# A retention and token-mixing kernel: 64-row PE tiles for two chunks at a time, in an explicit order of steps

## The chip, the cores and the metric

The kernel runs on one core of a Trainium2 chip. The metric is device time in microseconds (us) of one launch. A profile of one execution gives the span, engine times and waits. The timed figure of the profiled execution lies 1.7 to 1.8 us above its span, so spans are compared with spans and times with times.

Runs of one kernel differ by some per cent. The slower ones often show a lower clock granted to TensorE (PE), as with the changed kernel's 119.21 us at 0.927 of full clock against 114.94 us at 0.940, but not always: a fast run of e13, 115.26 us, had 0.888. Where the text says half clock, PE was granted half of its full clock for a while (0.50 from 30 to 35 us in the trace of the changed kernel). A run more than 1.5% above the fastest of the same kernel is labelled slow.

## The reference, cut to what matters

```python
# q, k, v: (B=4, H=8, S=768, D=64) float32
gamma = 1.0 - 2.0 ** (-5.0 - np.arange(H))
for t in range(S):                                   # retention with decay
    state = gamma * state + outer(k[:, :, t], v[:, :, t])
    y[:, :, t] = (1 / sqrt(D)) * q[:, :, t] @ state
x  = y as (B, S, H * D)                              # 512 columns
wq, wk = x @ w_q, x @ w_k                            # 64 columns each
W_tok  = (1 / sqrt(64)) * einsum('bsd,btd->bst', wq, wk)
mixed  = einsum('bst,btd->bsd', W_tok, x)
return maximum(mixed, 0) @ w_out                     # (4, 768, 512)
```

Both kernels take the recurrence in chunks of 128 tokens. q is multiplied by gamma^t and k by gamma^-t; then each chunk is masked scores times v, plus q times the state of all earlier chunks. `mixed` is computed as wq (wk^T x), so z = wk^T x (64 x 512) comes first, once per batch, and no S x S matrix is formed.

## The kernel before

24 chunks, one after another, placed by a scheduler. One 256 KB load for each of q, k and v in a chunk, in rows of one head and one token:

```python
nc.sync.dma_start(
    out=q_st,                                        # [128 tokens, H, D] float32
    in_=q[b, :, c * C : (c + 1) * C, :].rearrange("h t d -> t h d"),
)
# ... k and v alike ...
nc.gpsimd.tensor_tensor(out=qs, in0=st["q_st"],
    in1=fq[:, c, :].to_broadcast([128, H, D]), op=ALU.mult)
# ... ks alike, on GpSimd ...
nc.scalar.activation(out=vs, in_=st["v_st"], func=ACT.Copy, scale=float(attn_scale))
```

Transposes (8 for a chunk), scores in two 64-row tiles, mask, state and output:

```python
for parity in range(2):
    ps = psum_pool.tile([128, 4, C], FP32, name="at_ps", tag="ps")
    for j in range(4):
        h = 2 * j + parity
        nc.tensor.matmul(out=ps[:, j, :], lhsT=kT(qkt, h), rhs=qT(qkt, h), ...)
# ... at_sb = at_ps * cmask on DVE, twice 128 x 512 ...
for hp in range(HP):                                 # both heads of a pair in one 128 x 128 product
    nc.tensor.matmul(out=state_ps[:, hp, :, :], lhsT=ks[:, 2*hp : 2*hp+2, :],
                     rhs=vs[:, 2*hp : 2*hp+2, :], ...)
nc.scalar.copy(out=u_tile[0:64, :, 0, :], in_=state_ps[0:64, :, 0, :])       # keep the two
nc.scalar.copy(out=u_tile[64:128, :, 1, :], in_=state_ps[64:128, :, 1, :])   # diagonal blocks
# ... y_ps: 4 matmuls qkt x u_tile, 8 matmuls at_sb x vs ...
```

The mixing stage of a batch (wq and wk products, z, mx, projection with w_out) is placed beside the attention of the next batch. All tiles in PSUM come from one pool of eight buffers.

## Time and profile before

| | before |
|---|---|
| time, median of 3 runs | 132.82 us (132.27 to 135.31) |
| span | 132.4 us |
| PE busy, matmuls | 97.8 us, 1128 |
| DVE, ACT, POOL busy | 78.6, 58.3, 50.9 us |
| packets of DMA | 79,933 |

Busy time of PE counts the modelled lengths of matmuls that overlap; it is not the time PE needs. For that one goes from start to start in the timeline, as the prediction does. Two lines that the prediction does not show matter later. The first is from the list of DMA queues (packets, MB, share of 16 engines), the second from the groups of instructions (line, engine, operation, tiles, count, then busy us and mean ns, then idle time before them):

```profile
q8 instruction: 9, 0.15, 0.4%
...
L221 DVE TENSOR_TENSOR at_sb<-at_ps,cmask 128x512 bf16<-128x512 f32 x48 | 31.0, 684 | 25.0 <-PE at_ps L211 25.0
```

Queue q8 is labelled "instruction": nine packets of 16 KB, 0.15 MB in all, while PE runs 2256 instructions.

### The profile page before, as it was taken

To read this page: it belongs to the slowest core of one execution; us is meant where nothing else is said; L and a number is where in the kernel's file an instruction comes from. 1 tells how busy PE (TensorE), PEld (TensorE's weight loads), DVE (VectorE), ACT (ScalarE), POOL (GpSimd) and SP (SyncE) were. 2 spreads that over 40 slices of the span, in tenths; PEclk is the share of its full clock that TensorE was granted. 3 is DMA by queue.
4 is the path that set the end of the run, shared out by engine and by line. 5 is a ranking of instruction groups with operands and counts; after the bars stand their busy time and mean duration, and the time that the engine had idled before them with its cause. 6 is when DMAs were issued, how large, how long until landed. Compare 5 with 4: busy or idle time off the path is not lost.

```text
span 132.4 us, 2906 instructions
## 1 busy us (share of the span) xinstructions
PE 97.8 (74%) x1128; PEld 64.1 (48%) x1128; DVE 78.6 (59%) x141; ACT 58.3 (44%) x127; POOL 50.9 (38%) x65
## 2 busy tenths in 40 slices
PE   0003679765699899981799899861999999977970
PEld 0002558544478466560476556541675556653320
DVE  4061654975767599393457797590637797551830
ACT  3002454653556645382315757362325657413430
POOL 4009755467627654240765550425754200000000
PEclk9999999999999999999779999998569999999999
DMA  3899999999979998959999839959998006600074
GB/s 83 289 272 247 240 245 228 225 246 246 270 168 229 240 226 261 237 168 272 254 244 251 196 83 303 251 172 268 260 223 197 0 4 235 241 0 0 5 296 179
DMA packets 79933, 26.66 MB, mean 201 GB/s; under 512 B 76336, under 2 KB 76336, under 8 KB 79920
## 3 DMA queue, kind: packets, MB, share of 16 engines
q1 hardware_dynamic: 79920, 26.48, 79.6%
q8 instruction: 9, 0.15, 0.4%
q14 instruction: 4, 0.03, 0.1%
HBM read 20.19 MB, written 6.29 MB: 200 GB/s over the span
## 4 chain that ended last, share of the span: by engine, by line
PE 52%; SPq 16%; DMA 13%; ACT 4%; DVE 4%; POOL 4%; issue 3%; POOLq 0%; ACTq 0%; DVEq 0%
PE o_ps L379 13%; DMA q_st<-in_q_dram 12%; SPq L142 6%; PE wqt_ps L308 6%; PE z_ps L342 5%; PE mx_ps L358 4%; PE at_ps L211 4%; SPq L134 4%; PE tr_ps L181 3%; PE xt_ps L285 3%; PE y_ps L269 3%; SPq L138 3%; POOL qs L156 3%; PE wk_ps L322 3%; PE y_ps L261 3%
## 5 line engine op out<-in xcount | busy, mean ns | idle before, releaser
L221 DVE TENSOR_TENSOR at_sb<-at_ps,cmask 128x512 bf16<-128x512 f32 x48 | 31.0, 684 | 25.0 <-PE at_ps L211 25.0
L156 POOL TENSOR_TENSOR qs<-q_st,fq 128x512 bf16<-128x512 f32 x24 | 25.0, 1042 | 48.2 <-DMA q_st<-in_q_dram 33.3
L276 ACT CAST x_nat<-y_ps 128x512 bf16<-128x512 f32 x24 | 14.0, 585 | 29.5 <-PE y_ps L269 29.4
L162 POOL TENSOR_TENSOR ks<-k_st,fk 128x512 bf16<-128x512 f32 x24 | 25.0, 1042 | 3.6 <-DMA k_st<-in_k_dram 2.5
L181 PE MATMUL tr_ps<-identity,qs 128*128 128x128 bf16 x96 | 10.5, 239 | 20.4 <-POOL qs L156 20.3
L379 PE MATMUL o_ps<-wout_sb,relu_mx 128*128 128x512 bf16 x96 | 22.4, 379 | 0.0
L199 DVE COPY qkt<-tr_ps 128x1024 bf16<-128x1024 bf16 x24 | 16.4, 681 | 4.3 <-PE tr_ps L190 4.3
L181 PEld LDWEIGHTS <-qs 128*128 128x128 bf16 x96 | 6.9, 106 | 23.7 <-POOL qs L156 21.6
L168 ACT ACTIVATE vs<-v_st 128x512 bf16<-128x512 f32 x24 | 15.2, 632 | 0.3 <-DMA v_st<-in_v_dram 0.3
L367 DVE TENSOR_SCALAR relu_mx<-mx_ps 128x512 bf16<-128x512 f32 x16 | 9.9, 683 | 8.0 <-PE mx_ps L358 8.0
L379 PEld LDWEIGHTS <-relu_mx 128*128 128x128 bf16 x96 | 8.9, 98 | 9.8 <-DVE relu_mx L367 1.1
L238 PE MATMUL state_ps<-vs,ks 128*128 128x128 bf16 x80 | 8.6, 232 | 4.8 <-ACT vs L168 2.8
L190 PE MATMUL tr_ps<-identity,ks 128*128 128x128 bf16 x96 | 10.7, 242 | 1.1 <-POOL ks L162 1.1
L269 PE MATMUL y_ps<-vs,at_sb 128*128 128x64 bf16 x192 | 11.1, 201 | 0.0
L247 ACT CAST u_tile<-state_ps 64x256 bf16<-64x256 f32 x20 | 7.3, 365 | 8.3 <-PE state_ps L238 8.3
L211 PE MATMUL at_ps<-qkt 64*128 64x128 bf16 x192 | 10.6, 233 | 0.4 <-DVE qkt L199 0.4
L285 PE MATMUL xt_ps<-identity,x_nat 128*128 128x128 bf16 x96 | 10.0, 228 | 1.2 <-ACT x_nat L276 1.1
L388 DVE COPY o_st<-o_ps 128x512 f32<-128x512 f32 x12 | 8.2, 686 | 3.8 <-PE o_ps L379 2.1
L390 ACT COPY o_st<-o_ps 128x512 f32<-128x512 f32 x12 | 7.0, 584 | 7.3 <-PE o_ps L379 5.7
L308 PE MATMUL wqt_ps<-x_t,wq_sb 128*64 128x256 bf16 x48 | 9.2, 342 | 0.3 <-DVE x_t L296 0.3
L238 PEld LDWEIGHTS <-ks 128*128 128x128 bf16 x80 | 5.9, 105 | 7.1 <-issue 7.0
L261 PE MATMUL y_ps<-u_tile,qkt 128*128 128x128 bf16 x80 | 9.3, 226 | 0.0
(37 smaller groups left out, 101.1 us busy)
## 6 DMA issues: line engine op xcount, KB each, us to landing
q_st<-in_q_dram SPq DMA_DIRECT2D x24, 256.0 KB, 4.3
k_st<-in_k_dram SPq DMA_DIRECT2D x24, 256.0 KB, 4.2
v_st<-in_v_dram SPq DMA_DIRECT2D x24, 256.0 KB, 4.3
out_dram<-o_st SPq DMA_DIRECT2D x24, 256.0 KB, 2.3
wout_stage<-in_moe_w_out_dram SPq DMA_DIRECT2D x1, 1024.0 KB, 5.9
wq_stage<-in_moe_w_q_dram SPq DMA_DIRECT2D x1, 128.0 KB, 2.2
wk_stage<-in_moe_w_k_dram SPq DMA_DIRECT2D x1, 128.0 KB, 2.4
```

Source lines behind the costliest of these rows:

```text
L156: nc.gpsimd.tensor_tensor(out=qs, in0=st["q_st"], in1=fq[:, c, :].to_broadcast([128, H, D]), op=ALU.mult,)
L162: nc.gpsimd.tensor_tensor(out=ks, in0=st["k_st"], in1=fk[:, c, :].to_broadcast([128, H, D]), op=ALU.mult,)
L168: nc.scalar.activation(out=vs, in_=st["v_st"], func=ACT.Copy, scale=float(attn_scale))
L181: nc.tensor.matmul(out=tr_ps[:, hp, :], lhsT=qs[:, 2 * hp : 2 * hp + 2, :], rhs=identity, is_transpose=True, start=True, stop=True,)
L199: nc.vector.tensor_copy(out=qkt, in_=tr_ps)
L211: nc.tensor.matmul(out=ps[:, j, :], lhsT=kT(qkt, h), rhs=qT(qkt, h), start=(j == 0), stop=(j == 3),)
L221: nc.vector.tensor_tensor(out=at_sb_par[:, parity, :, :], in0=at_ps[parity], in1=cmask.to_broadcast([128, 4, C]), op=ALU.mult,)
L238: nc.tensor.matmul(out=state_ps[:, hp, :, :], lhsT=ks[:, 2 * hp : 2 * hp + 2, :], rhs=vs[:, 2 * hp : 2 * hp + 2, :], start=(c == 0 and hp ...
L269: nc.tensor.matmul(out=y_ps[:, h, :], lhsT=at_sb[:, h, :], rhs=vs[:, h, :], start=(c == 0 and h == 0), stop=(h == H - 1),)
L276: nc.scalar.copy(out=x_nats[b][:, c, :], in_=y_ps)
L308: nc.tensor.matmul(out=wqt_ps, lhsT=wq_sb[:, dmc, :], rhs=x_t[:, dmc, blk * 2 * C : (blk + 1) * 2 * C], start=(dmc == 0), stop=(dmc == NDM ...
L379: nc.tensor.matmul(out=o_ps, lhsT=relu_mx[:, dmc, tc_i * C : (tc_i + 1) * C], rhs=wout_sb[:, dmc, :], start=(dmc == 0), stop=(dmc == NDM - 1),
```

## The change

The intent is larger load rows and fuller PE tiles. Two successive tokens of a head lie in one partition, so that a load row is 512 B instead of 256 B, and a step handles a pair of chunks (256 tokens). Scores, inter-chunk product and state run in four 64 x 64 tiles, the inner product in two row tiles. The scale of v goes into `wk_sb`. `wq_sb` is doubled so that both row halves of the result hold wq^T and mx can use two row tiles. Everything is placed by a list of tokens: `sc.1.0` is the scores of pair 1, first half; `:V`, `:A`, `:P` give DVE, ACT or GpSimd; `fill.80` puts 80 dummy transposes ahead of the next PE step, meant to keep the clock up.

```diff
-    stage_pool = ctx.enter_context(tc.tile_pool(name="stage", bufs=15))
-    psum_pool = ctx.enter_context(tc.tile_pool(name="psum", bufs=8, space=bass.MemoryType.PSUM))
+    ctx.enter_context(tc.manual_schedule())
+    stage_pool = pool("stage", STAGES)               # STAGES = 6, for each of k, q, v
+    at_psum = pool("at_psum", 1, space=PSUM)         # 4 KB a partition
+    y_psum = pool("y_psum", 1, space=PSUM)           # 4 KB a partition
+    s_psum = pool("s_psum", 1, space=PSUM)           # 1 KB a partition
+    psum = pool("psum", 3, space=PSUM)               # 3 buffers for all other products
 ... cut ...
-        nc.sync.dma_start(out=q_st,
-            in_=q[b, :, c * C : (c + 1) * C, :].rearrange("h t d -> t h d"))
+        eng = nc.scalar if (name, p) == ("k", 0) else nc.sync
+        eng.dma_start(out=t.rearrange("g h j d -> g h (j d)"),
+            in_=src[b, :, cp * 2 * C : (cp + 1) * 2 * C, :].rearrange(
+                "h (g j) d -> g h (j d)", j=2))
 ... cut ...
-        for parity in range(2):
-            for j in range(4):
-                nc.tensor.matmul(out=ps[:, j, :], lhsT=kT(qkt, h), rhs=qT(qkt, h), ...)
+        for hi in range(2):
+            for j in range(2):
+                for x in range(2):
+                    for c in range(2):
+                        nc.tensor.matmul(out=ps[rows(c), x, hi, j, :],
+                            lhsT=st["kT"][rows(x), hp, j, c, :],
+                            rhs=st["qT"][rows(x), hp, c, :], ...)
 ... cut: state and inter-chunk product in 64x64 tiles, taken in turns two by two ...
+    wq_sb = const_pool.tile([128, NDM, 2, DH], BF16, name="wq_sb")
+    wk_scale = (1.0 / math.sqrt(D)) ** 3 / math.sqrt(DH)
 ... cut ...
+ORDER = """
+fill.80 ck.0:V trk.0 cq.0:V ekT.0:A trq.0 cv.0:V fill.2 eqT.0:V
+st.0 es.0.0:A sc.0.0 X.0 eat.0.0:V es.0.1:A sc.0.1 ck.1:P ia.0.0
 ... cut: 39 more lines of tokens ...
+for token in ORDER:
+    ... steps[name](e, *args) ...
```

## The prediction

> **What bounds the kernel now.** I read the page first (engine shares, the 40 slices, the DMA part), then the table of waits, then the busy time by stretch, and last the timeline of PE, to price single matmuls. From the page:
>
> ```profile
> PE 97.8 (74%) x1128; PEld 64.1 (48%) x1128; DVE 78.6 (59%) x141; ACT 58.3 (44%) x127; POOL 50.9 (38%) x65
> ...
> DMA  3899999999979998959999839959998006600074
> ...
> DMA packets 79933, 26.66 MB, mean 201 GB/s; under 512 B 76336, under 2 KB 76336, under 8 KB 79920
> ```
>
> No engine is full, but the DMA digits stand at 9 for most of the first 31 slices (103 us), and 76336 of 79933 packets are under 512 B: q, k and v are fetched in rows of one head and one token, 64 floats or 256 B. The table of waits (engine and line, what it waited for, total us, times, longest) names the same transfer:
>
> ```profile
> POOL qs L156 <- DMA q_st<-in_q_dram: 33.3, 18, 5.6
> ACT x_nat L276 <- PE y_ps L269: 29.4, 22, 4.0
> DVE at_sb L221 <- PE at_ps L211: 25.0, 15, 3.9
> PEld L181 <- POOL qs L156: 21.6, 8, 11.2
> ```
>
> The decay multiply waits 33 us for q, PE waits 22 us for the decay, and DVE and ACT wait for PE: one chain that starts at the loads. Busy time by stretch (length; PE, PEld, DVE, ACT, POOL; clock; DMA share; GB/s):
>
> ```profile
> 20.00:30.00 10.00, 7.80 (x113) 6.20 (x112) 6.94 (x11) 5.54 (x12) 5.61 (x7) 1.00 1.03 233
> 30.00:40.00 10.00, 7.19 (x119) 5.55 (x118) 6.79 (x12) 4.81 (x10) 5.74 (x6) 1.00 1.01 228
> ...
> 120.00:132.00 12.00, 7.52 (x36) 2.99 (x34) 4.51 (x7) 3.69 (x8) 0.00 (x0) 1.00 0.35 132
> ```
>
> In the load phase the queues are full (share 1.03) at only 233 GB/s. At the end there are only stores, in 2 KB packets, and they move 132 / 0.35 = 377 GB/s per full share. So the kernel is **bound by loads in small packets** to about 103 us, then by a tail in which the last batch's mixing and projection run with nothing beside them. The timeline of PE in a stretch where PE was fed (start, length, engine, line, what):
>
> ```profile
> 46.30 0.40 PE L181 MATMUL tr_ps<-identity,qs 128*128 128x128 bf16 x4
> 46.63 0.41 PE L211 MATMUL at_ps<-qkt 64*128 64x128 bf16 x8
> 46.97 0.23 PE L261 MATMUL y_ps<-u_tile,qkt 128*128 128x128 bf16 x1
> 47.03 0.39 PE L190 MATMUL tr_ps<-identity,ks 128*128 128x128 bf16 x4
> 47.26 0.33 PE L261 MATMUL y_ps<-u_tile,qkt 128*128 128x128 bf16 x3
> 47.43 0.40 PE L269 MATMUL y_ps<-vs,at_sb 128*128 128x64 bf16 x8
> 47.66 0.38 PE L379 MATMUL o_ps<-wout_sb,relu_mx 128*128 128x512 bf16 x1
> ```
>
> Lengths overlap, so prices come from start to start. From 46.97 to 47.43 there are 8 matmuls of N=128: 57 ns each. From 47.43 to 47.66 there are 8 of N=64: 29 ns each. The 8 scores, in two 64-row tiles, take 46.63 to 46.97 = 0.34 us: four pairs at 57 ns (0.23) plus 0.11 of something else, and likewise 46.30 to 46.63 is four transposes (0.23) plus 0.10. The projection (12 in 2.59 us in the chain) is 216 ns at N=512.
>
> [...]the extra 0.10 us on either side of the scores[...] so I price a **mode change at 0.095 us**.[...] Nothing in this trace runs matmuls in four 64x64 tiles, so their price is my largest unknown.[...] The trace has 256 B and 2 KB packets[...] but it has no 512 B packet.
>
> **The change part by part.**
>
> *Loads.* Two successive tokens of a head lie in one partition, so a row is 512 B. 18.87 MB of q, k, v becomes 36,900 packets instead of 73,700. Before, a packet of 256 B cost 256 x 16 / 226 (233 / 1.03) = 18.1 ns of an engine, one of 2 KB 2048 x 16 / 377 = 86.9 ns. A line through both gives 27.9 ns at 512 B, or 293 GB/s[...]. I take 330: loads need 57 us (50 to 64) against 83, a pair of chunks (1.57 MB) lands every 4.8 us, and the weights (1.3 MB, behind pair 2) cost 3.5 us. Stores (6.3 MB, 17 us) mostly come later. DMA falls to about 78 us of work.
>
> *PE.* The new order has 2032 matmuls and 100 warm-up fills against 1128. Counted per pair of chunks, 12 pairs:
> - transposes 24 x 57 ns = 1.37 us, as before (288 in both);
> - scores 32 in 64x64 tiles, N=128; inter-chunk 27 and state 27, N=64. If weight loads of the four tiles pass at the 14 ns that separate the score pairs (57 / 4), 86 x 14 = 1.20 us.[...] Middle 1.75;
> - inner product 32, in two row tiles, 14.5 ns each = 0.46;
> - wqk 4 x 110 + 8 x 29 = 0.67; z and mx 8 x 57 = 0.46; projection 8 x 216 = 1.73;
> - mode changes: 98 in the token order, 8.2 a pair x 0.095 = 0.78.
>
> Sum 7.2 us a pair (6.7 to 7.8), **87 us in all (80 to 93)**. The same sum for before is 75 us of matmuls plus some 72 mode changes = 82. So PE gets no lighter: tiling pays only in z and mx, and small stationaries and mode changes eat it.
>
> *Other engines.* Mask multiplies go from 48 of 684 ns to 24 of twice the width, about 1.23 us (413 ns at 256 columns and 684 at 512 give 1.06 ns a column): 29 us. With its share of copies DVE comes to about 67 us (78.6 now), ACT 60 (58.3), and POOL, with 22 decays of about 2.05 us (twice 1042 ns) and 5 copies, 50. None bounds. Folding the scale of v into wk and doubling wq only free the choice of engine and fill both row halves.
>
> *The path.* First data after about 6 us, PE starts near 7 (11.2 now). Until k of pair 4 is there the loads set the pace: 2.5 + 4 x 4.8 + 3.5 + 1.6 = 27 us, 29 after decay and transposes. By then PE has done three pairs of attention, part of the fourth and batch 0's first mixing, about 17 us. The remaining 70 us of PE run with data at hand: 99. Last eviction, store and end: 132.4 - 128.2 = 4 us as now. That is 103 without stalls. The tail of batch 3 shrinks, because its first two pairs are transposed and projected beside attention. Some 2 us for stalls at the three shared PSUM banks and the end: **105 us**.
>
> **Rivals.**
> 1. *Loads still bind* (512 B at 256 B speed per byte, 226 GB/s): 84 us of loads plus weights and a 12 us tail, 103 to 112. The rate rise from 256 B to 2 KB[...] speak against it.
> 2. *Fast four-tile issue* (14 ns or less): PE 80 us, end near 96. For it: the scores already start 14 ns apart. Against: those have 128-column stationaries.
> 3. *PSUM becomes the bound.* Transposes, xT, wqk, z, mx and projection, 100 bank uses in all, share three banks where eight served everything. A use of about 0.6 matmul, 0.7 eviction and 0.8 latency and queueing is 2.1 us, x 100 / 3 = 70 us: just under PE. If ACT and DVE lag, PE stalls 10 us: 115.
> 4. *The fixed order stalls at a late transfer* and every engine behind it waits: 110 to 120. The six stages (half the input in flight) speak against it.
>
> **Range and chances.** The load rate moves the early phase by 5 us each way, the four-tile price PE by 6, PSUM stalls by up to 10, upward only. Together 96 to 116. A result above 130 needs two rivals at full size, so faster 0.97, same 0.02, slower 0.01.
>
> **What would show it.** Load packets of 512 B taking 22 to 28 ns; DMA share high only to about 65 us; PE with few gaps after 30 us; start-to-start of scores and state between 14 and 27 ns; 0.1 us at each mode change; DVE near 67, ACT 60, POOL 50 busy. It is wrong if PE still waits for loads after 40 us, if four-tile matmuls take over 30 ns or under 12, or if PE's gaps end at evictions and sum to more than 10 us.

## The result, and the profile after

| | before | after |
|---|---|---|
| time, median of 4 runs | 132.92 us (132.27 to 135.31) | 116.22 us (114.94 to 119.21) |
| span of the profiled run | 132.4 us | 114.7 us |
| ratio of fast runs | | 0.8734 (0.8662 to 0.8806) |

A ratio is the mean time of one kernel's fast runs over that of the other's in the same rounds, so it is not quite the ratio of the medians. The kernel takes 12.7% less time. The result is correct. It lies 11 us above the predicted time and just above the top of the range.

The page of the changed kernel, first its busy times, then the slices and the DMA lines:

```profile
span 114.7 us, 4693 instructions
...
PE 94.7 (83%) x2118; PEld 69.5 (61%) x2132; DVE 65.0 (57%) x87; ACT 60.3 (53%) x94; POOL 49.7 (43%) x41
...
PE   3977596993789899997994949999999999978830
...
PEclk9999958999558999999999995899999999999998
DMA  1999999999999989999999999993421004422472
...
DMA packets 40916, 26.77 MB, mean 233 GB/s; under 512 B 1856, under 2 KB 38720, under 8 KB 40896
...
q8 instruction: 16, 0.26, 1.0%
...
L324 DVE TENSOR_TENSOR at_sb<-at_ps,cmask 128x1024 bf16<-128x1024 f32 x24 | 29.3, 1222 | 10.8 <-PE at_ps L311 10.6
```

A slice is 2.87 us. The DMA digits stand at 9 up to some 77 us instead of 103 (the last packet of a load row ends at 75.9 us instead of 102.7). Loads that end 27 us sooner fit the expected cause of the gain. No run puts the old rows into the new kernel or the new rows into the old one, so how the 16 us divide between rows, tiles and order is not shown. Packets have halved. DVE, ACT and POOL are within 2 us of what was predicted, and the mask multiply takes 1222 ns (1.23 us predicted). But the PE digits dip to 3 and 7 near 30 us and to 4 near 60 and 66 us, where PE was to run with data at hand; the clock digits drop to 5 in three places; and there are 16 packets of instructions instead of 9.

The table of waits (engine, tile and line, what it waited for; total us, times, longest):

```profile
POOL ks L248 <- DMA k_st<-in_k_dram: 16.6, 9, 6.6
...
PEld L311 <- issue: 6.7, 9, 1.7
PEld L380 <- issue: 4.8, 12, 1.7
PE at_ps L311 <- DVE at_sb L324: 2.4, 3, 1.1
```

GpSimd still waits for loads, but PE's large waits are no longer for GpSimd: they are "issue", time in which the engine waited for nothing that the profile shows, up to 1.7 us at once. (Weight loads overlap matmuls, 69.5 and 94.7 us busy in a span of 114.7 us, so not all of the 6.7 and 4.8 us is lost.) The timeline of PE around three of the four longest stalls:

```profile
25.76 0.35 PE L311 MATMUL at_ps<-qT,kT 64*64 64x128 bf16 x8
27.62 0.27 PE L311 MATMUL at_ps<-qT,kT 64*64 64x128 bf16 x5 [1.50 <-issue]
...
61.30 0.41 PE L487 MATMUL z_ps<-x_nat,wqk_sb 128*64 128x256 bf16 x3
63.11 0.73 PE L487 MATMUL z_ps<-x_nat,wqk_sb 128*64 128x256 bf16 x9 [1.41 <-issue]
...
66.54 0.32 PE L380 MATMUL state_ps<-vs,ks 64*64 64x64 bf16 x9
68.49 0.21 PE L380 MATMUL state_ps<-vs,ks 64*64 64x64 bf16 x1 [1.62 <-issue]
```

Each stall falls in the middle of a step, between two matmuls whose operands were all there before the step began. No buffer or bank changes hands at that point.

I split PE's time in this trace into the price of each matmul at full clock, mode changes, the surplus at half clock, and the rest. (14 of 96 projection matmuls have no record; their 3.0 us are put back.)

| part of the span | predicted | measured |
|---|---|---|
| first stretch | to 29 us, 17 us of PE work done | cut at 29.2 us, 11.6 us done |
| PE work after it | 70 | 67.1 |
| losses after it | 2 | 13.8 |
| after the last matmul | 4 | 4.7 |
| span | 105 | 114.8 |

The cut at 29.2 us is the end of the last mask of pair 2; I chose it afterwards, to split the span. The event that the prediction put at 29 us is another one: k of pair 4, decayed and transposed. Its decay ended at 34.2 us and its transposes began at 37.5, so that the two numbers agree is a coincidence.

The 13.8 us of losses after 29.2 us are: stalls such as those above, three of them (at 52.4, 63.1 and 68.5 us), 4.5 us; half clock 3.7 us; waits for relu and z in the last batch 1.3 us; and some 4.3 us scattered. Before 29.2 us PE waited 3.75 us for mask multiplies and 1.67 us at the stall at 27.6 us, and lost 1.5 us to half clock; the rest of that stretch is the start and waits for data.

### Where the stalls fall

PE's stream has 2132 matmuls and as many weight loads, 4264 instructions, against 2256 before. Numbering them in order in the raw trace, and taking the times of the 16 KB packets of queue q8, gives this for the changed kernel:

```
packet of instructions    PE resumes at    number of the instruction (as recorded)
25.27 to 26.29            27.62             961
49.64 to 50.81            52.37            1981
60.51 to 61.69            63.11            2491
65.77 to 66.94            68.49            2747
```

With the missing matmul records counted in, the last three become 1985, 2497 and 2753. All four leave 193 on division by 256. A packet has 16,384 B and the stalls lie 256 apart or a multiple of it, so I take one packet for one block of 256 instructions, 64 B each. The counts agree: 16 packets for 4264 instructions of PE (266 each), 9 for 2256 before (251 each). So the theory that I tested, **F**: PE stalls at the edge of a block of 256 instructions, because the next block has not come, while loads fill the DMA queues.

A crossing of such an edge cost up to 1.8 us here. In all 17 traces together, PE has 45 pauses of 0.9 us or more, from start to start, for which the profile names no releaser. All 45 lie at such an edge, and each ends 1.3 to 1.7 us after the end of a packet of q8. The kernel before has none: a block lasted it 10.8 to 16.4 us.

From all traces I read the pace of these blocks: when PE enters a block, the packet of the next one starts 2.6 us later by the median while loads run (somewhat over half within 1.9 to 3.2 us, all within 0.1 to 4.5), and 0.6 us later when they are done (two thirds within 0.4 to 1.3 us); it lasts about 1.2 us; and the block is usable no sooner than some 1.3 us after the packet's end. My estimate from these: a block must last about 2.6 + 1.2 + 1.3 = 5.1 us while loads run, some 40 ns for a matmul with its weight load, or 0.6 + 1.2 + 1.3 = 3.1 us when they don't. In the load phase PE took mostly 5 to 6 us a block (median 5.4): at the limit. Matmuls in four 64x64 tiles follow one another at 8 to 13 ns, so a block of those runs out early.

### The profile page after: what moved, and what is told of

The parts are those of the page before. It is cut to its first block, busy times and chain, and to the rows that moved or that the text cites.

```text
span 114.7 us, 4693 instructions
## 1 busy us (share of the span) xinstructions
PE 94.7 (83%) x2118; PEld 69.5 (61%) x2132; DVE 65.0 (57%) x87; ACT 60.3 (53%) x94; POOL 49.7 (43%) x41
## 3 DMA queue, kind: packets, MB, share of 16 engines
q1 hardware_dynamic: 39856, 25.96, 78.4%
## 4 chain that ended last, share of the span: by engine, by line
PE 70%; DVE 10%; issue 8%; DMA 5%; ACT 3%; DVEq 0%; ACTq 0%
PE o_ps L533 19%; PE at_ps L311 8%; PE y_ps L417 6%; PE xt_ps L440 6%; PE wqk_ps L455 6%; DVE at_sb L324 6%; PE qtr_ps L294 6%; DMA k_st<-in_k_dram 5%; PE y_ps L380 5%; PE z_ps L487 3%; PE ktr_ps L280 3%; PE wqk_ps L465 3%; PE mx_ps L509 3%; PE state_ps L380 2%; DVE qs L248 1%
## 5 line engine op out<-in xcount | busy, mean ns | idle before, releaser
L324 DVE TENSOR_TENSOR at_sb<-at_ps,cmask 128x1024 bf16<-128x1024 f32 x24 | 29.3, 1222 | 10.8 <-PE at_ps L311 10.6
L248 POOL TENSOR_TENSOR ks<-k_st,fk 128x1024 bf16<-128x1024 f32 x11 | 20.9, 1902 | 22.3 <-DMA k_st<-in_k_dram 16.6
L533 PE MATMUL o_ps<-wout_sb,relu 128*128 128x512 bf16 x82 | 23.9, 389 | 1.2 <-ACT o_st L127 0.3
L248 POOL TENSOR_TENSOR qs<-q_st,fq 128x1024 bf16<-128x1024 f32 x11 | 20.9, 1902 | 2.6 <-DMA q_st<-in_q_dram 2.6
L127 ACT COPY o_st<-o_ps 128x512 f32<-128x512 f32 x19 | 11.2, 587 | 10.8 <-PE o_ps L533 10.5
L311 PE MATMUL at_ps<-qT,kT 64*64 64x128 bf16 x384 | 11.0, 226 | 5.2 <-issue 2.5
L533 PEld LDWEIGHTS <-relu 128*128 128x128 bf16 x96 | 8.4, 99 | 8.3 <-issue 1.7
L524 ACT ACTIVATE relu<-mx_ps 128x512 bf16<-128x512 f32 x18 | 10.2, 598 | 3.3 <-PE mx_ps L509 2.6
L380 PE MATMUL y_ps<-s_sb,qT 64*64 64x64 bf16 x320 | 9.8, 197 | 1.0 <-DVE at_sb L324 1.0
L380 PE MATMUL state_ps<-vs,ks 64*64 64x64 bf16 x320 | 9.1, 197 | 1.6 <-issue 1.6
L417 PE MATMUL y_ps<-vs,at_sb 64*128 64x64 bf16 x384 | 10.0, 193 | 0.3 <-DVE at_sb L324 0.2
```

What stands on the lines that cost most here:

```text
L127: return nc.scalar.copy(out=out, in_=in_)
L248: ENGINES[e].tensor_tensor(out=st[name + "s"].rearrange("p hp j x d -> p x (hp j) d"), in0=st[name + "_st"].rearrange("p (x hp) j d -> p x ...
L311: nc.tensor.matmul(out=ps[rows(c), x, hi, j, :], lhsT=st["kT"][rows(x), hp, j, c, :], rhs=st["qT"][rows(x), hp, c, :], start=(hi == 0 and ...
L324: st["eat", half] = ENGINES[e].tensor_tensor(out=st["at", half].rearrange("p x hi j t -> p (x hi) (j t)"), in0=st["at_ps", half].rearrange ...
L380: out.append(nc.tensor.matmul(skip_group_check=True, **mm))
L417: nc.tensor.matmul(out=st["y_ps"][:, c, x, hp, :], lhsT=st["at", half][rows(c), x, hi, j, :], rhs=st["vs"][rows(c), hp, j, x, :], start=(( ...
```

## The experiments

The expectations name theories by letters. F is the one above. L: the loads hold PE up for their data, and with them gone PE runs through. P: what holds PE is on PE itself or in its PSUM banks, and does not change with the loads. C: the first 29 us are set by a chain of decay, transpose, scores and mask multiply alone. D: the stalls are waits of particular steps for data or an eviction that the profile did not name. Times are medians; ratios are against the kernel before, in the same rounds. The traces of e4, e5, e6, e8, e9, e10 and e11 are of slow executions; they are used for where PE stops, not for how long the kernel takes.

### e1_half_loads: without the later loads

Pairs 6 to 11 use the staged tiles of pairs 0 to 5 again. The result is wrong; all work on the engines stays.

```diff
         if p + STAGES < NG:
-            load(name, p + STAGES)
+            pairs[p + STAGES][name + "_st"] = pairs[p][name + "_st"]
```

> q, k and v of pairs 6 to 11 are not loaded; the staged tiles of pairs 0 to 5 are used again (wrong result on purpose). Theory F (instruction blocks of 16 KB for PE come late because the 16 DMA engines are full of loads; in the changed kernel PE stood 1.1 to 1.8 us at 27.6, 52.4, 63.1 and 68.5 us, each time at a multiple of about 255 instructions in its stream and about 1.4 us after the end of a 16 KB packet): the loads end near 40 us, the three stalls after that are gone (4.5 us), so is the half-clock stretch at 69.4 to 72.8 (1.5 us), and the stall near 27 us stays: 108 to 110 us. Theory L (the late loads themselves hold PE back): the attention of pairs 6 to 11 starts as early as its order allows and the time falls to 100 us or less. Theory P (three PSUM banks and evictions): no change, 115 to 116.

Measured: 109.81 us, ratio 0.8226 (0.8173 to 0.8278), span 108.3. Busy time by stretch (length; PE, PEld, DVE, ACT, POOL; clock; DMA share; GB/s), first of the changed kernel, then of this run:

```profile
60.00:65.00 5.00, 3.55 (x136) 2.90 (x133) 2.97 (x5) 2.27 (x6) 4.15 (x3) 1.00 1.13 291
65.00:70.00 5.00, 3.38 (x102) 2.63 (x100) 3.20 (x6) 1.93 (x3) 4.31 (x3) 0.94 1.10 296
70.00:75.00 5.00, 4.78 (x63) 2.80 (x61) 2.77 (x4) 1.76 (x4) 2.03 (x3) 0.72 1.11 344
```

```profile
60.00:65.00 5.00, 5.00 (x193) 4.25 (x190) 4.68 (x7) 3.00 (x5) 5.00 (x4) 1.00 0.02 5
65.00:70.00 5.00, 5.00 (x103) 3.33 (x96) 4.29 (x6) 2.89 (x6) 5.00 (x3) 1.00 0.02 7
70.00:75.00 5.00, 5.00 (x112) 3.00 (x110) 5.00 (x7) 3.04 (x5) 1.29 (x2) 1.00 0.27 107
```

With a DMA share of 0.02 to 0.27, PE has no idle time at all and the clock stays at 1.00. From 60 to 65 us it passes 193 matmuls, so 386 instructions, in 5 us: more than a block. The late stalls are gone, the one at instruction 961, in the load phase, is still there, and half clock fell from 5.2 to 2.2 us. The 6.4 us of span are about what 4.5 us of stalls and 3.0 us of half clock make, less 1.4 us by which two stalls before 29 us grew. F is confirmed. L (100 us or less) and P are refuted: no PSUM bank was touched. In the kernel unaltered PE was behind its data at this time (k of pair 8 was ready at 57.3 us and used at 64 to 65), so these are not waits for data.

### e2_rows_4k: the same bytes in rows of 4 KB

Each load reads 128 rows of 4 KB. The values land in the wrong places, so the result is wrong; bytes, loads and engine work are the same.

```diff
-            out=t.rearrange("g h j d -> g h (j d)"),
-            in_=src[b, :, cp * 2 * C : (cp + 1) * 2 * C, :].rearrange("h (g j) d -> g h (j d)", j=2),
+            out=t.rearrange("g h j d -> g (h j d)"),
+            in_=src.rearrange("b h s d -> (b h s d)")[
+                p * 128 * H * 2 * D : (p + 1) * 128 * H * 2 * D].rearrange("(g x) -> g x", g=128),
```

> The same bytes in the same number of DMAs, but in rows of 4 KB (a contiguous block per partition, wrong result on purpose), so a DMA engine moves them at the rate of the stores (4096 B in 159 ns, 412 GB/s) instead of 29 ns for 512 B (281 GB/s). A pair lands every 4 us instead of 5.7. Theory F: shorter load phase (to about 52 us), fewer late instruction blocks; the stalls at 63 and 68 us vanish, and the first 30 us of PE work, which wait for pair after pair, gain 3 to 5 us: 105 to 109. Theory L: about 100. Theory P: 115. If fetch stalls depend on full queues whatever the packet, those before 50 us stay.

Measured: 113.33 us, ratio 0.8436 (0.8364 to 0.8509). That misses what F expected. The page shows 400 to 420 GB/s instead of about 290, and the loads end near 56 us. The stalls at 63 and 68 us are gone, as F says, but one of 1.85 us at 53.1 us remains and half clock is 5.6 us. The last mask of pair 2, which ends the first stretch, was done at 28.4 us instead of 29.2: loads 40% faster bought at most 0.8 us there (a second trace of the changed kernel, e9, has 30.2, so single traces differ by as much). One thing that took their place is a cast of weights. The timeline of DVE, then of POOL:

```profile
22.67 0.61 DVE L128 CAST wq_sb<-wq_stage 128x512 bf16<-128x512 f32 x1
23.20 1.99 DVE L226 TENSOR_SCALAR wk_sb<-wk_stage 128x256 bf16<-128x256 f32 x1
```

```profile
22.95 2.08 POOL L248 TENSOR_TENSOR qs<-q_st,fq 128x1024 bf16<-128x1024 f32 x1
25.00 1.95 POOL L248 TENSOR_TENSOR ks<-k_st,fk 128x1024 bf16<-128x1024 f32 x1
```

The wk cast takes 286 ns in the changed kernel's own trace and 1987 ns here, where it began during a decay on GpSimd and ended just after it; PE waited 1.2 us for it. The same holds in all traces of the new order: in the three where the cast began during a decay (e2, e6, e8) it took 1985 to 1987 ns, in the 13 others 284 to 289. So the slow casts are those that began during a decay on GpSimd; why, the traces do not show.

### e3_fill48 and e4_fill16: the block edges moved through the work

With fewer dummy transposes at the start the same steps get lower instruction numbers: by 64 with 48 fills, by 128 with 16. Both results are correct.

```diff
-fill.80 ck.0:V trk.0 cq.0:V ekT.0:A trq.0 cv.0:V fill.2 eqT.0:V
+fill.48 ck.0:V trk.0 cq.0:V ekT.0:A trq.0 cv.0:V fill.2 eqT.0:V
```

> 48 warm-up fills ahead of the first transposes instead of 80: the PE stream is 64 instructions shorter ahead of all work, and nothing else changes. PE waited 0.75 us for the first decayed k after the fills, so the start does not move. Theory F: the stalls stay at the same place in the count of PE instructions (about 961, 1981, 2491, 2746), which is 64 instructions (32 matmuls) later in the work, in other steps; their number and size change a little: 113 to 118 us. Theory D (they are waits of those steps for data or an eviction that the profile did not name): they stay at the same matmuls and so come 64 earlier in the count.

> 16 fills instead of 80, so 128 instructions (half a block of 256) are taken away ahead of all work. Theory F: stalls at the same counts again, half a block later in the work, 112 to 118 us; the clock may be half at the first transposes[...] (about 1 us). Theory D: the stalls stay at the same matmuls, 128 earlier in the count.

Measured: 114.97 us, ratio 0.8603 (0.8547 to 0.8659), and 114.4 us (112.19 to 117.37), ratio 0.8448 (0.8352 to 0.8543) from two fast runs. The longest stalls fell at numbers 2241 and 2497 in e3 and at 705 and 2497 in e4; the shorter ones of e3 (0.8 us at 2753, 0.7 at 3777) are at edges too. Around 2497 the timeline of PE shows, for e3 and then for e4:

```profile
61.04 0.19 PE L380 MATMUL state_ps<-vs,ks 64*64 64x64 bf16 x1
62.81 0.21 PE L380 MATMUL state_ps<-vs,ks 64*64 64x64 bf16 x1 [1.58 <-issue]
```

```profile
61.69 0.56 PE L280 MATMUL ktr_ps<-identity,ks 128*128 128x128 bf16 x7
64.88 0.23 PE L280 MATMUL ktr_ps<-identity,ks 128*128 128x128 bf16 x1 [2.62 <-issue]
```

In e3 the stall splits two state products, in e4 the last of eight transposes from the other seven. The later runs have one at the same number too:

| run | number 2497 falls in |
|---|---|
| e3_fill48 | state |
| e4_fill16 | transposes of k |
| e13_fill32_only | transposes of x |
| e14_no_fills | inter-chunk product |
| e15_no_mid_fills | scores |

The place stays at one count of instructions and moves through the work. A cause in a step, a buffer or a bank would stay with the step: D is refuted, and F's forecast came true.

### e5_split_mask and e6_split_mask_4k: half of the early masks moved to ACT

For pairs 0 to 2 DVE masks half of the scores and ACT copies the other half unmasked. This is C's test; e6 adds the 4 KB rows of e2. Their outputs are wrong, which doesn't matter for the times.

```diff
+        nx = 1 if p < 3 else 2
-            out=st["at", half].rearrange(...), in0=st["at_ps", half].rearrange(...),
+            out=st["at", half][:, 0:nx].rearrange(...), in0=st["at_ps", half][:, 0:nx].rearrange(...),
+        if nx == 1:
+            nc.scalar.copy(out=st["at", half][:, 1], in_=st["at_ps", half][:, 1])
```

> In pairs 0 to 2 the mask multiply is halved: DVE takes one half of the heads, and ACT copies the other half unmasked at the same time (wrong result on purpose), so the step from scores to the inner product takes about 0.69 us instead of 1.22. Theory C (the first 29 us are set by the chain scores, mask, scores, mask of one pair after another, for which the order has nothing to put beside; PE waited 3.75 us for masks there): PE reaches the end of pair 2 some 2.5 to 3.5 us sooner, and the time falls by 1 to 3 us against the changed kernel, to 112 to 115, because k of pair 3 (cast by 27.8) then binds. Theory L (the loads pace the first 29 us): no change, 115 to 116.

> The halved mask step of e5_split_mask together with the 4 KB rows of e2_rows_4k (wrong result on purpose). Theory C: chain and loads each hide the other, so both together gain more than the sum: 107 to 110, against 113.3 with the rows alone. If neither matters in that phase: 112 to 113.

Measured: e5 115.77 us (113.58 to 116.25), with one fast run only and so no ratio: inconclusive. In its trace, of a slow execution, the last mask of pair 2 is done at 28.7 us (29.2 and 30.2 in the two traces of the changed kernel), where C expected 2.5 to 3.5 us sooner. e6 112.01 us, ratio 0.84 (0.8292 to 0.8508), which misses the 107 to 110 expected. In e6 PE waited 1.4 us for the wq cast and 1.3 us for the wk cast at 23 to 27 us. Shorter masks and faster loads together hand the wait to the next in line.

### e7_order and e8_order_wout: another order for the first pairs

e7 puts the transposes of k of pairs 2 and 3 ahead of a wait for a mask. e8 also loads w_out one pair later. Both are correct.

```diff
-X.1 es.1.1:A sc.1.1 cq.2:P trk.2 eat.1.1:V ...          ck.3:P Y.2 ia.2.1 ex.2:A cq.3:P trk.3 ...
+X.1 es.1.1:A trk.2 sc.1.1 cq.2:P eat.1.1:V ...          ck.3:P trk.3 Y.2 ia.2.1 ex.2:A cq.3:P ...
 e8 also:
-wqk.1 WO:A ew.0:V ...     exT.2:V cv.3:A ...            (w_out loaded behind pair 2)
+wqk.1 ew.0:V ...          exT.2:V WO:V cv.3:A ...       (w_out loaded behind pair 3)
```

> Correct kernel. 48 fills as in e3_fill48, and two tokens moved so that PE has transposes to do while it waits for a mask: k of pair 2 is transposed ahead of the second scores of pair 1, k of pair 3 ahead of the inter-chunk product of pair 2. Theory C: 0.5 and 1 us of waiting filled, 113 to 114.5 against 115.0 of e3_fill48. Theory F adds noise of one stall (1 to 2 us) either way, as the block boundaries fall on other steps.

> Correct kernel. As e7_order, and the load of w_out (1 MB, 3.6 us of the queues) goes behind pair 3 instead of pair 2, its cast to DVE after xT of pair 2. k of pair 3 lands 3.6 us sooner. Theory C with loads close behind: 112 to 114. If loads never matter in that phase: as e7_order within 0.5 us. It is slower if w_out then holds DVE ahead of the mask of pair 3.

Measured: e7 115.8 us, ratio 0.8695 (0.8581 to 0.8809), no gain over e3 with the same 48 fills. e8 118.29 us, ratio 0.8816 (0.866 to 0.8973). In e7 the earlier transpose met data that had not come, as the timeline of PE shows:

```profile
28.37 0.62 PE L280 MATMUL ktr_ps<-identity,ks 128*128 128x128 bf16 x8 [1.42 <-POOL ks L248]
```

PE then waited another 1.11 us for x. In e8, in the trace of a slow execution, PE waited 1.3 us for wk, had three stalls at block edges and some 8 us of half clock. So C is not confirmed: no single link sets the first 29 us. The mask chain, the loads close behind, the casts of weights and the clock each take over when another is eased. How they share that stretch stays open.

### e9_again: the changed kernel once more

> The changed kernel unaltered, as the base of the three runs beside it: 115 to 117 us, ratio to before 0.87. Every theory expects the same. In the load phase each block of 256 PE instructions again takes at least 5 us: the packet starts 1.9 to 3.2 us after the block before is entered, lasts 1.2, and the block is used no sooner than 1.3 us after that.

Measured: 116.71 us (115.78 to 118.19), ratio 0.8686 (0.8596 to 0.8776), on another chip than e1 to e4. It shares its rounds with the three runs that follow. Mean of its fast runs: 115.84 us. Its trace has blocks of 5.0 to 9.1 us while loads run, as expected; the next packet starts 0.3 to 4.3 us after a block is entered, a wider range than expected.

### e10_pad_loads and e11_pad_tail: one block more, in two places

128 tiny matmuls (64 x 64 tiles, 16 columns), so 256 instructions, whose values the scores then overwrite. Both results are correct. e10 puts 16 ahead of each score step of pairs 4 to 7, in the load phase; e11 puts 32 ahead of each of pairs 10 and 11, when loads are done.

```diff
+        for i in range(16 if 4 <= p < 8 else 0):         # e11: range(32 if p >= 10 else 0)
+            x, c = i % 2, i // 2 % 2
+            nc.tensor.matmul(out=ps[rows(c), x, 0, 0, 0:16],
+                lhsT=st["kT"][rows(x), 0, 0, c, :], rhs=st["qT"][rows(x), 0, c, 0:16],
+                start=True, stop=True, skip_group_check=True)
```

> 128 tiny matmuls (64x64 tiles, 16 columns, 256 instructions, one block) are added, 16 ahead of each score step of pairs 4 to 7, that is between 38 and 66 us while loads run; the result stays correct. Their own time at 14 ns each is 1.8 us. Theory F (PE is close to the supply limit of 256 instructions per 5.1 us while loads run): 3 to 6 us more than e9_again. If only PE's own time counts: 1.5 to 2 us more.

> The same 128 tiny matmuls, 32 ahead of each score step of pairs 10 and 11, between 80 and 96 us when the loads are done and a block starts to come 0.4 to 1.3 us after the block before is entered (limit about 3.2 us a block). Theory F: 1.8 to 3 us more than e9_again, clearly less than e10_pad_loads. If only PE's own time counts: 1.5 to 2 us, the same as e10_pad_loads.

Measured: e10 120.98 us, ratio 0.9001 (0.8817 to 0.9184), 4.2 us above e9_again by the means of fast runs. e11 118.58 us, ratio 0.879 (0.8672 to 0.8908), 1.4 us above it. Each mean rests on two or three fast runs. In the trace 16 of these matmuls take 0.15 us, so 128 make about 1.2 us: my estimate of their own price. In the tail they cost little more than that, somewhat under F's 1.8 to 3 us. In the load phase the same instructions cost some 3 us more, as F expected: e10's trace has seven stalls of 0.5 us or more, 9.1 us in all, two of them inside the added matmuls, against four and 6.8 us in e9's. In the tail the added block is not free either (stalls of 0.8 and 1.5 us at 89.6 and 93.6 us in e11's trace). The intervals of the two ratios overlap, so the difference in time is likely and not shown.

### e12_stages3: half the staging buffers

```diff
-STAGES = 6
+STAGES = 3
```

> Three staging buffers for each of q, k and v instead of six, so the load of pair p+3 waits for the cast of pair p. In the changed kernel a buffer was free long before its next load was issued (v of pair 8 cast at 66 us, v of pair 11 issued at 68.4), so the loads should run as before: within 1 us of e9_again. If the depth of the queue is what delays the instruction blocks, stalls shrink and it is 2 to 4 us faster; if loads are held back, it is slower.

Measured: 116.76 us, ratio 0.8675 (0.855 to 0.88), the same as e9_again. So six buffers are not needed. Whether the depth of the queue of loads delays the instructions stays open: this run hardly changed it, since between 25 and 70 us both traces have 0.4 to 1.2 MB of loads issued and not yet moved.

### e13_fill32_only, e14_no_fills, e15_no_mid_fills: what the fills are worth

e13 keeps 32 fills at the start and none later, e14 has none, e15 keeps the 80 and drops the 20 later ones. All are correct.

```diff
 e14:
-fill.80 ck.0:V trk.0 cq.0:V ekT.0:A trq.0 cv.0:V fill.2 eqT.0:V
+ck.0:V trk.0 cq.0:V ekT.0:A trq.0 cv.0:V eqT.0:V
 ... and fill.6, fill.4, fill.4, fill.4 removed further on ...
```

> Correct kernel: 32 fills ahead of the first transposes, and none of the 20 later ones, so 136 instructions fewer than the changed kernel. Theory F: half a block less to fetch, and e3_fill48 and e4_fill16 already ran at 115.0 and 114.4; 113 to 115, ratio to before 0.84 to 0.86. If the later fills hold the clock up, their loss costs 1 to 2 us of half clock near 15 to 35 us: 115 to 117.

> Correct kernel without any of the 100 fills (200 instructions fewer). Theory F: another quarter block less, but PE starts its work at half clock; 113 to 116. If the clock at the start matters more than the fetch: 116 to 118.

> Correct kernel: the first 80 fills kept, the 20 later ones gone (40 instructions fewer), to part the two. If the later fills are only instructions to fetch: 114.5 to 116. If they hold the clock: 116 to 118 with longer half-clock stretches before 36 us.

Measured: e13 116.0 us, ratio 0.8608 (0.8559 to 0.8657). e14 114.13 us (113.16 to 117.86), ratio 0.8497 (0.845 to 0.8544). e15 115.39 us (112.54 to 116.91), one fast run only and no ratio: inconclusive. The page of e14:

```profile
PE 88.1 (79%) x2032; PEld 62.9 (56%) x2032; DVE 64.9 (58%) x87; ACT 60.2 (54%) x94; POOL 49.5 (44%) x41
...
PE   0009698798659899999599929999999999969930
```

PE starts in the fourth slice instead of the first. Its first transposes run at half clock, 107 ns instead of 57, until about 24 us, and yet the last mask of pair 2 is done at 30.0 us, against 29.2 and 30.2 in the two traces with the fills. The record of the clock begins at 24.5 us in this trace and stays at full to the last matmul (before it the page's digits read 9 while the transposes ran at half speed, so those digits are not to be trusted there). So the fills earn nothing that the runs show, and **by fast runs e14 beats both kernels**: 0.8497 against 0.8734 and 0.8686 for the changed kernel, with intervals that do not overlap, though they come from different sessions and the record's own verdict is "unclear". e4, with 16 fills, is level with it (0.8448). Why it gains is not settled: 200 instructions fewer, the block edges in other places (1985 and 2497), and the clock all changed at once. Nor do the runs settle why the clock halves: e14 has stalls of 1.4 and 2.4 us and no half clock after them. The digit 2 near 66 us is such an edge.

## Why the prediction was right or wrong

**The direction and its reason were right.** The trace before shows full queues in 256 B packets and a chain that starts at the loads; after it the loads end 27 us sooner. That fits the reason given, though no run changes the rows alone. Load packets took 29 ns (31.0 on average) against 27.9 from the line through two sizes. I set that line aside for 330 GB/s, 25 ns, an estimate between the line's 293 GB/s and the 377 of the 2 KB packets; the line was right. A pair landed every 5.7 us, not 4.8. The times of DVE, ACT and POOL and the 0.095 us of a mode change (100 of them, 9.5 us) came out as said: from start to start a change took mostly 120 ns after an inner product and 149 ns after a transpose, against 26 ns from one pair of inner products to the next and 57 from transpose to transpose. The size was read from the extra 0.10 us beside the scores in the trace before. Matmuls of 128 and 512 columns in 128x128 tiles came 57 and 216 ns apart in both kernels.

**The price of four tiles was too high.** Scores came at 13.4 ns, state and inter-chunk products together at 8.2, alone at 16.4; I had 20 in the middle, an estimate: of the range around it only the lower end, 14 ns, came from a trace. PE work was 78.7 us, not 87. This helped by 8 us. Rival 2 had the price right, and the prediction's own sign of being wrong (four-tile matmuls under 12 ns) came true, but the end near 96 us that the rival drew from it did not. That 67.1 us of work were left after the cut, near the predicted 70, is luck: 8 us less work in all and 5.4 us less done by then nearly cancel. The lower price also made PE eat its instructions faster, which I did not see.

**The stretch to 29 us held less work.** I put 17 us of PE work into it and 11.6 were done. Its end at 29.2 us is no hit: k of pair 4, whose arrival the prediction let end it, was decayed only at 34.2 us. That did not stop PE, which came to it 3.3 us later still. PE waited for masks, for one block of instructions and at half clock. e2, e5, e6, e7 and e8 show that easing one of the links alone moves the end of it little.

**The step that failed** is "The remaining 70 us of PE run with data at hand: 99", with "Some 2 us for stalls at the three shared PSUM banks and the end". PE did have its data, and 67.1 us of work were left, but the losses were 13.8 us instead of 2. Of these 4.5 us are stalls at block edges and 3.7 us half clock; with the late loads gone (e1) both shrink and the span falls by 6.4 us. What halves the clock, and the 4.3 us of scattered losses, stay open. The sum counted 2032 + 100 matmuls by their time alone. It had no term for bringing 4264 instructions through the same DMA engines that the loads fill (q8's packets and the loads' queue q1 take 1.0% and 78.4% of the same 16 engines' span), and none for the clock. The doubling of instructions stood in the change. In the list of queues only the packet count of q8 hints at it.

The predicted sum was also a span, to be compared with 114.7 us; as a time it lacks 1.75 us. In all: 105 + 0.2 (first stretch) - 2.9 (less work) + 11.8 (losses) + 0.7 (end) = 114.8 us of span, and 1.75 more is 116.5, the profiled run's 116.46.

**The rivals.** Loads still bind (1): in part, after 29 us through the instructions rather than the data; before it PE also waits for data. PSUM (3): no; e1 gained 6 us without touching a bank, and the 0.8 us of latency and queueing in that sum was an estimate that no run tested. The fixed order stalled by a late transfer (4): not after the first stretch.

## What to carry to other kernels

Count instructions as well as time: where PE's stream is made of many small matmuls and loads fill the DMA queues, divide the PE time by the blocks of 256 instructions, and when a block takes about 5 us or less, look for stalls at its edges. The figure is from this one case: 10.8 to 16.4 us a block had none, 5 to 6 us had them. A stall marked "issue" in the middle of a step is checked by its instruction number: if it stays at one remainder of 256 while the work moves, as it did here at 193, suspect the supply of instructions. Warm-up fills add instructions too (200 for 100 fills here), so time the kernel without them before keeping them.

## What the traces add

- Beside full DMA queues the crossing of a block edge stalled PE for 0.9 to 2.8 us, one to six times in a run, 6.2 us in the changed kernel (4.5 of them after 29 us). How many instructions PE can hold no run shows, but the traces show only one block of 256 fetched ahead: in the changed kernel each of the 16 packets starts 0.4 to 4.3 us after PE has entered the block before it.
- While loads run, the packet of an instruction block starts 2.6 us after the block before it is entered by the median of all traces, against 0.6 us when the loads are done.
- Matmuls of 64 columns in four 64x64 tiles, each with its own weight load, followed one another at 8.2 ns, so some 32 ns apart within one tile, against 29 ns in the 128x128 tiles of the kernel before. No run compares the two with all else equal.
- Packets of 512 B took 29 ns, those of 2 KB 84 ns and those of 4 KB 159 ns, which over 16 engines is 282, 390 and 412 GB/s.
